# Pooled attention feeding a four-expert layer: two token blocks in one PSUM bank, double-buffered attention sums, an earlier q, plain products in the first chunk, merged last stores

## The chip, the cores and the metric

The kernel runs on one core of a Trainium2 chip. The metric is the device time of one execution in microseconds (us). Each experiment was timed beside runs of the kernel before on the same chip. Engines are named as the profile names them: PE is TensorE, PEld its weight loads, DVE is VectorE, ACT is ScalarE, POOL is GpSimd, SP is SyncE. A "q" behind an engine's name (SPq) is that engine issuing a DMA, and L452 is line 452 of that run's kernel. A DMA *lands* when the trace reports its completion. The *granted clock* is the share of its full speed at which TensorE was allowed to run, as the profile records it; 0.5 is called half clock here.

## The reference, cut to what matters

```python
# q, k, v: (8 batches, 8 heads, 576 tokens, 64)   x: (4608, 512)   w1: (4, 512, 1024)   w2: (4, 1024, 512)
k_p = k.reshape(B, H, 72, 8, D).mean(axis=3)          # keys and values pooled by 8: 72 of each
v_p = v.reshape(B, H, 72, 8, D).mean(axis=3)
attn = softmax(q @ k_p.T / sqrt(D))
x = (attn @ v_p).transpose(0, 2, 1, 3).reshape(4608, 512)
p = domain_probs / (domain_probs.sum(-1, keepdims=True) + 1e-09)
for e in range(4):
    out += p[:, e:e + 1] * (np.maximum(x @ w1[e], 0) @ w2[e])
```

The arithmetic of the four experts dwarfs the attention. The kernel walks through nine chunks of tokens: the first 512 tokens of each of the eight batches, then one chunk of all the remainders (8 times 64 tokens). Each chunk passes through four experts. One chunk and one expert make one *step*. While the experts work on chunk b, the attention of batch b+1 is mixed in as small *pieces*.

## The kernel before: the parts that matter here

The pools. PSUM has one attention buffer of two banks (`psum_a`), two banks for the up product, and four tags `o0` to `o3` of one bank each for the down product:

```python
hpool  = ctx.enter_context(tc.tile_pool(name="hpool", bufs=2))
psum_a = ctx.enter_context(tc.tile_pool(name="psum_a", bufs=1, space=bass.MemoryType.PSUM))
psum_h = ctx.enter_context(tc.tile_pool(name="psum_h", bufs=2, space=bass.MemoryType.PSUM))
psum_o = ctx.enter_context(tc.tile_pool(name="psum_o", bufs=1, space=bass.MemoryType.PSUM))
```

Per step the *up product* is 8 groups of four 512-column matmuls, each followed by a ReLU on ScalarE. The *down product* is a seven-product scheme (in the manner of Strassen): 56 matmuls of 256 columns in place of 32 of 512. It needs sums of the hidden values (`S1` to `S4`) and, once per expert, sums of the weights; VectorE makes both. VectorE also adds each product, weighted by the token's probability, into `acc`:

```python
def weight_sums(e):                       # four VectorE instructions, in the first chunk
    combine(t[:, 0], b12, ALU.subtract, b11)
    combine(b12, b22, ALU.subtract, b12)
    combine(t[:, 1], b22, ALU.subtract, t[:, 0])
    combine(t[:, 2], b21, ALU.subtract, t[:, 1])

def down(c, e, step):                     # step 0..6: one of the seven products, two token blocks each
    ...
    for j in range(BANKS):
        tag = f"o{int(chain[1]) + j}"     # each token block has its own bank
        if not grows:
            state[tag] = psum_o.tile([P, NT], F32, tag=tag, name="o_ps")
        o_ps = state[tag][:, 0:HD]
        for i in range(HF):
            nc.tensor.matmul(o_ps, lhsT=lhs[:, i, j * P:(j + 1) * P], rhs=rhs[:, i, :],
                             start=(not grows and i == 0), stop=(i == HF - 1), ...)
        ...
        nc.vector.scalar_tensor_tensor(out=dst, in0=o_ps, scalar=prob, in1=dst,
                                       op0=ALU.mult, op1=ALU.add)     # right after its block
        if e == E - 1 and step in (5, 6):
            store(c, r)

def store(c, r):
    if c < B:
        ...
    else:                                 # the last chunk: two batches of 64 tokens in each block
        for bb in range(2):
            at = (2 * r + bb) * S + NT
            nc.sync.dma_start(out=out[at:at + REM, :], in_=acc[bb * REM:(bb + 1) * REM, r, :])
```

The start. TensorE runs filler matmuls on zeros (`idle`) while it waits for k and q, both cast to bf16 on the way by software DMA from GpSimd:

```python
load_k(0); load_q(0); load_v(0); load_w1(0); load_probs(); load_w1(1); ...    # all on GpSimd

def attention_first():
    idle(14)
    sum_keys(lo)
    idle(2)
    keys(0, lo)
    idle(8)
    sum_keys(hi)
    idle(2)
    keys(0, hi)
    for pair in range(NPAIR):
        queries(0, pair)
        if pair:
            scores(0, pair - 1)
    ...
```

The attention pieces of later batches end with the turn of x into the layout that the up product reads, by DMA transpose; the loads of the next batch are issued by GpSimd once the keys of this one are there (`gate`):

```python
def turn(b, r):
    if b:
        nc.sync.dma_start_transpose(out=state[("xT", b)][:, :, r * P:(r + 1) * P], in_=x_tok)
        return
    ...                                   # batch 0: four transposes on TensorE, copied by ScalarE

def next_loads(b):
    nc.gpsimd.tensor_copy(out=gate[0:1, 0:1], in_=state[("kpT", b)][0:1, 0, 0:1])
    load_q(b + 1); load_k(b + 1); load_v(b + 1); load_q_rem(b + 1)
```

The main loop, one step after the other: the up product of step s beside the down product of step s−1.

```python
for s in range(len(steps) + 1):
    ...
    for i in range(FCH):
        if 0 < s < len(steps):
            up(c, e, (i,))
        if s > 0 and i < 7:
            down(*steps[s - 1], i)
        slot()                            # now and then: one attention piece
        if s < len(steps) and i == HF:
            early_sum(c, e)
        if (s, i) in ((0, 6), (1, 5), (3, 0), (3, 6)):
            weight_sums(...)
```

The softmax here doesn't subtract the row's maximum and nothing guards it: scores larger than these inputs give would overflow.

Of the kernel before, what the change touches and what calls it, by code (L numbers as in the profile page):

```python
# [9 lines left out]
ACT = mybir.ActivationFunctionType  # L10
ALU = mybir.AluOpType
# [6 lines left out]
def kernel(  # L18
# [36 lines left out]
    hpool = ctx.enter_context(tc.tile_pool(name="hpool", bufs=2))  # L55
    spool = ctx.enter_context(tc.tile_pool(name="spool", bufs=1))

    psum_a = ctx.enter_context(tc.tile_pool(name="psum_a", bufs=1, space=bass.MemoryType.PSUM))
# [35 lines left out]
    def load_q(b):  # L94
        q_sb = qpool.tile([P, H, NR, D], BF16, name="q_sb")
        for hs in groups(b):
            nc.gpsimd.dma_start(  # L97
                out=q_sb[:, hs].rearrange("p h r d -> p h (r d)"),
                in_=q[b, hs, 0:NT, :].rearrange("h (p r) d -> p h (r d)", r=NR),
            )  # L100
        raws[("q", b)] = q_sb
# [60 lines left out]
    def spare_bank():  # L162

        turns[0] += 1
        return psum_o.tile([P, NT], F32, tag=f"o{turns[0] % 4}", name="spare")
# [80 lines left out]
    def scores(b, pair):  # L246
        qT = state[("qT", b)]
        if pair == 0:
            state[("expT", b)] = apool.tile([SP, H, 2, 2, P], BF16, name="expT")
        expT = state[("expT", b)]  # L250
        banks = two_banks(b == 0 and pair % 2)
        for hh in range(2):
            h = 2 * pair + hh
            for r2 in range(2):
                lo = r2 * D
                nc.tensor.matmul(  # L256
                    banks[r2][:, hh * 2 * P:(hh + 1) * 2 * P],
                    lhsT=key_columns(b, h, lo), rhs=qT[lo:lo + D, h],
                )
        exp_out = expT[:, 2 * pair:2 * pair + 2].rearrange("j h a b t -> j b (h a) t")  # L260
        for sc, r2 in whole(banks):
            nc.scalar.activation(  # L262
                out=exp_out[:, r2], in_=sc[0:SP].rearrange("j b (g t) -> j b g t", t=P),
                func=ACT.Exp, scale=EXP_SCALE,
            )

    def one_bank(b):
        return spare_bank()[:] if b == 0 else two_banks(False)[0]

    def two_banks(spare):  # L270
        if spare:
            return [spare_bank()[:], spare_bank()[:]]
        t = psum_a.tile([P, 2, NT], F32, tag="a", name="a_ps")
        return [t[:, 0], t[:, 1], t]

    def whole(banks):

        if len(banks) == 3:
            return [(banks[2][:], slice(0, 2))]
        return [(banks[i].unsqueeze(1), slice(i, i + 1)) for i in range(2)]  # L280

    def divide(banks, x_tok):

        for ps, hs in whole(banks):
            n = hs.stop - hs.start
            c = ps[:, :, 0:NPAIR * (D + 1)].rearrange("p a (h d) -> p a h d", d=D + 1)
            inv = npool.tile([P, 2, NPAIR], F32, name="inv")
            nc.vector.reciprocal(out=inv[:, 0:n], in_=c[:, :, :, D])  # L288
            nc.vector.tensor_tensor(  # L289
                out=x_tok[:, hs], in0=c[:, :, :, 0:D],  # L290
                in1=inv[:, 0:n].unsqueeze(3).to_broadcast([P, n, NPAIR, D]), op=ALU.mult,
            )

    def context(b, r):
        expT, vp = state[("expT", b)], vps[b % 3]
        x_tok = npool.tile([P, 2, NPAIR, D], BF16, name="x_tok", bufs=4)
        banks = two_banks(b == 0 and r % 2)
        for h in range(H):
            at = h % NPAIR * (D + 1)
            nc.tensor.matmul(  # L300
                banks[h // NPAIR][:, at:at + D + 1],
                lhsT=expT[:, h, r // 2, r % 2, :], rhs=vp[:, h, :],
            )
        divide(banks, x_tok)
        state[("x", b, r)] = x_tok
# [40 lines left out]
    def rem_context(i):  # L346
        expTr = state.pop(("expTr", i))
        x_tok = npool.tile([P, 2, NPAIR, D], BF16, name="x_tok", bufs=4)
        banks = two_banks(False)
        for h in range(H):  # L350
            at = h % NPAIR * (D + 1)
            for bb in range(2):
                nc.tensor.matmul(  # L353
                    banks[h // NPAIR][bb * REM:(bb + 1) * REM, at:at + D + 1],
                    lhsT=expTr[:, h % 2, bb, h // 2, :], rhs=vps[(2 * i + bb) % 3][:, h, :],
                )
        divide(banks, x_tok)
        state[("xr", i)] = x_tok
# [7 lines left out]
    def attention_first():  # L366

        lo, hi = groups(0)
        idle(14)
        sum_keys(lo)  # L370
        idle(2)
        keys(0, lo)
        idle(8)
        sum_keys(hi)
        idle(2)
        keys(0, hi)
        for pair in range(NPAIR):
            queries(0, pair)
            if pair:
                scores(0, pair - 1)  # L380
        scores(0, NPAIR - 1)
        idle(1)
# [19 lines left out]
    def attention(b):  # L402
# [15 lines left out]
        for pair in range(NPAIR):  # L418
            pieces.append(lambda pair=pair: scores(b, pair))
# [48 lines left out]
    BANKS = 2  # L468
# [35 lines left out]
    def down(c, e, step):  # L504
# [3 lines left out]
        if step == 0:  # L508
            hidden_sums(c, e)
        chain, grows, lhs, rhs, row, col, first = [  # L510
            lambda: ("o0", 0, a11, w[:, LO, 0:HD], 0, 0, True),
            lambda: ("o2", 0, a12, w[:, HI, 0:HD], 0, 0, False),
            lambda: ("o0", 1, state["S2"], t[:, 1], 0, 1, True),
            lambda: ("o2", 0, state["S1"], t[:, 0], 1, 1, True),
            lambda: ("o0", 1, state[("S3", c, e)], w[:, LO, HD:DM], 1, 1, False),
            lambda: ("o2", 1, state["S4"], w[:, HI, HD:DM], 0, 1, False),
            lambda: ("o0", 1, a22, t[:, 2], 1, 0, True),
        ][step]()
        for j in range(BANKS):
            tag = f"o{int(chain[1]) + j}"  # L520
            if not grows:
                state[tag] = psum_o.tile([P, NT], F32, tag=tag, name="o_ps")
            o_ps = state[tag][:, 0:HD]
            for i in range(HF):
                nc.tensor.matmul(  # L525
                    o_ps, lhsT=lhs[:, i, j * P:(j + 1) * P], rhs=rhs[:, i, :],
                    start=(not grows and i == 0), stop=(i == HF - 1),
                    skip_group_check=True,
                )
            r = row * BANKS + j  # L530
            prob = p_all[:, c * NR + r, e:e + 1]
            dst = acc[:, r, col * HD:(col + 1) * HD]
            if e == 0 and first:
                nc.scalar.activation(out=dst, in_=o_ps, func=ACT.Copy, scale=prob)  # L534
            else:
                nc.vector.scalar_tensor_tensor(  # L536
                    out=dst, in0=o_ps, scalar=prob, in1=dst, op0=ALU.mult, op1=ALU.add,
                )
            if e == E - 1 and step in (5, 6):
                store(c, r)  # L540
        if step == 1:
            last_sum(c, e)

    def store(c, r):
# [3 lines left out]
        else:  # L548
            for bb in range(2):
                at = (2 * r + bb) * S + NT  # L550
                nc.sync.dma_start(out=out[at:at + REM, :],
                                  in_=acc[bb * REM:(bb + 1) * REM, r, :])
# [11 lines left out]
    steps = [(c, e) for c in range(NCH) for e in range(E)]  # L564
    SLOTS = E * FCH


    ENG = mybir.EngineType
    with tc.manual_schedule(engines={ENG.PE, ENG.DVE, ENG.Activation, ENG.Pool, ENG.SP}):
        load_k(0)  # L570
        load_q(0)
        load_v(0)
        load_w1(0)
        load_probs()
        load_w1(1)
        load_w2(0)
        load_w1(2)
        load_w2(1)
        attention_first()
# [3 lines left out]
        load_w1(3)  # L583
# [16 lines left out]
        for s in range(len(steps) + 1):  # L600
            if s < len(steps):
                c, e = steps[s]
                if e == 0:
                    while pieces:
                        pieces.popleft()()
                    pieces.extend(attention(c + 1) if c + 1 < B else
                                  rem_pieces(c // 2) if c < B else [])

                    late = SLOTS // 2 - 1 if c == 0 else 0
                    per_slot = len(pieces) / (SLOTS - 3 - late)  # L610
                    due = -late * per_slot
            for i in range(FCH):
                if 0 < s < len(steps):
                    up(c, e, (i,))
                if s > 0 and i < 7:
                    down(*steps[s - 1], i)
                slot()
                if s < len(steps) and i == HF:
                    early_sum(c, e)

                if (s, i) in ((0, 6), (1, 5), (3, 0), (3, 6)):
                    weight_sums({(0, 6): 0, (1, 5): 1, (3, 0): 2, (3, 6): 3}[(s, i)])
# [30 lines left out]
```

## Time and profile before

| quantity | value | read from |
|---|---|---|
| device time, median | 539.25 us (538.17 to 540.45, 4 runs) | times |
| span of the profiled run, mean granted clock | 537.5 us, 0.992 | list of cores |
| PE busy | 516.9 us, 96% | page, part 1 |
| start of the first up product | 22.17 us | timeline |
| second up product to second chunk | 30.58 to 84.16 us | trace, first weight load of each up product |
| last accumulate ends, span ends | 530.92, 537.5 us | timeline |

The profile page of the kernel before: busy time, the granted clock in 40 equal slices, and the chain of work that ended last.

```profile
span 537.5 us, 9393 instructions
...
PE 516.9 (96%) x3839; PEld 335.5 (62%) x3839; DVE 365.2 (68%) x745; ACT 238.3 (44%) x413; POOL 41.6 (8%) x59
...
PEclk9999989999999999999999999999999999999998
...
PE 85%; DMA 8%; DVE 4%; POOL 1%; ACT 1%; issue 0%; DVEq 0%; POOLq 0%
```

TensorE bounds the kernel. The windows view of the same kernel says where. Its columns are the stretch (start and end, length), busy us and instructions of PE, PEld, DVE, ACT and POOL, then the granted clock, the mean number of busy DMA packets divided by 16 engines (packets overlap, so it can pass 1), and GB/s.

```profile
8.00:16.00 8.00, 6.62 (x61) 3.75 (x59) 2.98 (x8) 2.44 (x5) 3.63 (x6) 1.00 1.28 188
16.00:24.00 8.00, 6.93 (x84) 5.56 (x81) 5.44 (x17) 4.46 (x10) 3.37 (x5) 1.00 1.18 213
71.77:75.19 3.42, 1.50 (x18) 0.92 (x16) 3.39 (x9) 0.00 (x0) 0.00 (x0) 1.00 1.70 101
75.19:78.61 3.42, 3.42 (x14) 1.82 (x12) 1.67 (x4) 0.60 (x1) 0.00 (x0) 0.50 1.40 105
84.50:140.40 55.90, 55.90 (x434) 35.98 (x432) 42.16 (x85) 26.64 (x45) 3.84 (x5) 1.00 0.51 85
140.40:195.30 54.90, 54.90 (x402) 35.60 (x400) 39.26 (x79) 25.88 (x45) 4.43 (x5) 1.00 0.41 69
195.30:251.10 55.80, 55.80 (x433) 35.99 (x432) 40.28 (x81) 26.92 (x45) 3.44 (x5) 1.00 0.50 83
531.00:537.50 6.50, 0.00 (x0) 0.00 (x0) 0.00 (x0) 0.00 (x0) 0.00 (x0) 0.62 0.69 160
```

Three chunks in the middle keep PE busy every microsecond at full clock. Only the ends have slack: the start, the first chunk (with one stretch at half clock, right after a stretch in which PE was busy 1.50 of 3.42 us), and the tail, in which only DMA works, at a busy share of 0.69.

What TensorE waits for in the whole run of the kernel before (waiting engine, tile and line, then what it waited for, us in total, times, longest):

```profile
PE a_ps L300 <- DVE x_tok L289: 1.9, 1, 1.9
PE a_ps L237 <- DMA q_sb<-in_q_dram: 1.8, 1, 1.8
PE a_ps L237 <- DVE qT L240: 1.8, 2, 1.3
```

The first three stand in the first chunk; two of them exist because the attention sums have one buffer. The timeline of the kernel before, four rows from start and end (start, us, engine and line, what; in brackets the idle time before it and what ended that):

```profile
1.20 6.00 PE L215 MATMUL w_ps<-zeros 128*128 128x512 bf16 x14 [1.20 <-DVE zeros L556]
7.04 1.04 PE L199 MATMUL s_ps<-kraw,ident 72*72 72x256 bf16 x8
...
22.17 1.03 PE L452 MATMUL h_ps<-xT,w_bf 128*128 128x256 bf16 x8 [0.41 <-ACT xT L318]
...
529.77 5.03 SPq L551 DMA_DIRECT2D out_dram<-acc  x8
```

At the end SyncE needs 5.03 us to issue eight stores.

### The profile page before, as it was taken

How to read it: one execution, taken by the hardware profiler on the slowest of the kernel's cores; microseconds unless marked ns; L12 is line 12 of the kernel's file. 1: busy time of each engine (PE TensorE's matmuls, PEld its weight loads, DVE VectorE, ACT ScalarE, POOL GpSimd, SP SyncE). 2: the span in 40 equal slices, each digit the busy share in tenths (PEclk: the TensorE clock that was granted, in tenths of full speed). 3: DMA queues.
4: the chain of work that ended last, by engine and by line, in shares of the span. 5: the costliest groups of instructions: out<-in, count | busy, mean ns of one | idle time of the engine just before them, and what ended most of it. 6: DMA issues, size and time to landing. Idle time of an engine off the chain costs nothing.

```text
span 537.5 us, 9393 instructions
## 1 busy us (share of the span) xinstructions
PE 516.9 (96%) x3839; PEld 335.5 (62%) x3839; DVE 365.2 (68%) x745; ACT 238.3 (44%) x413; POOL 41.6 (8%) x59
## 2 busy tenths in 40 slices
PE   8897989999999999999999999999999999999993
PEld 4664556666665666566656665666566666666663
DVE  2548678867775778477937785778477636763665
ACT  1662523563356335633473347333743364336330
POOL 7410200200030000200300002000000000000000
PEclk9999989999999999999999999999999999999998
DMA  8999993491265134913491329331001110011003
GB/s 124 209 208 206 201 113 60 111 123 31 50 142 82 29 61 91 136 28 59 102 124 21 68 78 129 49 60 59 32 15 27 45 44 2 11 39 40 2 1 78
DMA packets 73419, 41.52 MB, mean 77 GB/s; under 512 B 44688, under 2 KB 67216, under 8 KB 73376
## 3 DMA queue, kind: packets, MB, share of 16 engines
q0 software_dynamic: 32032, 22.63, 29.7%
q1 hardware_dynamic: 41344, 18.29, 15.3%
q8 instruction: 30, 0.49, 0.4%
q14 instruction: 13, 0.11, 0.1%
HBM read 45.16 MB, written 9.44 MB: 102 GB/s over the span
## 4 chain that ended last, share of the span: by engine, by line
PE 85%; DMA 8%; DVE 4%; POOL 1%; ACT 1%; issue 0%; DVEq 0%; POOLq 0%
PE h_ps L452 43%; PE o_ps L525 38%; DMA kraw<-in_k_dram 4%; DMA w_bf<-in_moe_w_dram 3%; PE a_ps L256 2%; PE a_ps L300 1%; DVE acc L536 1%; DMA x_rem<-x_tok 0%; ACT expT L262 0%; DVE wt_bf L471 0%; POOL q_sb L97 0%; PE a_ps L353 0%; POOL kraw L89 0%; POOL vraw L89 0%; DVE x_tok L289 0%
## 5 line engine op out<-in xcount | busy, mean ns | idle before, releaser
L456 ACT ACTIVATE H_sb<-h_ps 128x512 bf16<-128x512 f32 (+1 forms) x296 | 173.2, 585 | 253.1 <-PE h_ps L452 252.7
L452 PE MATMUL h_ps<-xT,w_bf 128*128 128x512 bf16 (+1 forms) x1056 | 260.4, 374 | 0.7 <-ACT xT L318 0.4
L536 DVE SCALAR_TENSOR_TENSOR acc<-o_ps,p_all,acc 128x256 f32<-128x256 f32 x432 | 194.1, 481 | 96.0 <-PE o_ps L525 78.6
L452 PEld LDWEIGHTS <-w_bf 128*128 128x128 bf16 x1184 | 110.9, 98 | 86.8 <-issue 8.0
L525 PEld LDWEIGHTS <-H_sb 128*128 128x128 bf16 x864 | 84.5, 98 | 32.5 <-DMA w_bf<-in_moe_w_dram 0.4
L525 PE MATMUL o_ps<-w_bf,H_sb 128*128 128x256 bf16 x576 | 74.5, 273 | 0.0
L525 PE MATMUL o_ps<-wt_bf,H_sb 128*128 128x256 bf16 x288 | 37.3, 273 | 0.0
L262 ACT ACTIVATE expT<-a_ps 72x1024 bf16<-72x1024 f32 x30 | 30.5, 1017 | 13.7 <-PE a_ps L256 13.7
L452 PE MATMUL h_ps<-x_rem,w_bf 128*128 128x512 bf16 x128 | 32.4, 379 | 0.8 <-DMA x_rem<-x_tok 0.8
L534 ACT ACTIVATE acc<-o_ps,p_all 128x256 f32<-128x256 f32 x72 | 31.3, 472 | 3.9 <-DMA out_dram<-acc 3.4
L289 DVE TENSOR_TENSOR x_tok<-a_ps,inv 128x512 bf16<-128x512 f32 x34 | 23.5, 691 | 1.2
L300 PEld LDWEIGHTS <-expT 72*128 72x128 bf16 x256 | 12.3, 98 | 4.4 <-DVE x_tok L289 2.2
L215 PE MATMUL w_ps<-zeros 128*128 128x512 bf16 x31 | 10.8, 489 | 1.2 <-DVE zeros L556 1.2
L429 POOL COPY gate<-kpT_101 1x1 bf16<-1x1 bf16 x2 | 1.4, 708 | 102.1 <-DMA kpT_101<-kp_99 55.5
L288 DVE RECIPROCAL inv<-a_ps 128x8 f32<-128x8 f32 x34 | 6.7, 198 | 3.5 <-PE a_ps L300 3.1
L168 DVE TENSOR_TENSOR kraw<-kraw 72x2048 bf16<-72x2048 bf16 x7 | 8.5, 1212 | 0.3 <-DMA kraw<-in_k_dram 0.3
L168 DVE TENSOR_TENSOR vraw<-vraw 72x2048 bf16<-72x2048 bf16 x7 | 8.5, 1211 | 0.0
L429 POOL COPY gate<-kpT_103 1x1 bf16<-1x1 bf16 x2 | 1.9, 934 | 84.8 <-DMA kpT_103<-kp_100 45.2
L300 PE MATMUL a_ps<-vp_105,expT 72*128 72x65 bf16 x96 | 5.1, 194 | 3.0 <-DVE x_tok L289 1.9
L97 POOL DMA_DIRECT2D q_sb<-in_q_dram x9 | 7.8, 868 | 1.4 <-issue 1.1
L89 POOL DMA_DIRECT2D kraw<-in_k_dram x9 | 7.6, 842 | 3.9 <-DMA p_all<-in_moe_domain_probs_dram 3.4
L89 POOL DMA_DIRECT2D vraw<-in_v_dram x9 | 7.3, 810 | 1.8 <-DVE vp_105 L220 1.8
(513 smaller groups left out, 484.8 us busy)
## 6 DMA issues: line engine op xcount, KB each, us to landing
out_dram<-acc SPq DMA_DIRECT2D x32, 256.0 KB, 2.6
w_bf<-in_moe_w_dram POOLq DMA_DIRECT2D x7, 1024.0 KB, 23.8
kraw<-in_k_dram POOLq DMA_DIRECT2D x7, 576.0 KB, 11.6
vraw<-in_v_dram POOLq DMA_DIRECT2D x7, 576.0 KB, 13.4
q_sb<-in_q_dram POOLq DMA_DIRECT2D x7, 512.0 KB, 8.3
w_bf<-in_moe_w_dram POOLq DMA_DIRECT2D x2, 512.0 KB, 13.0
out_dram<-acc SPq DMA_DIRECT2D x8, 128.0 KB, 2.3
kraw<-in_k_dram POOLq DMA_DIRECT2D x2, 288.0 KB, 5.8
```

The source lines that it names most:

```text
L89: nc.gpsimd.dma_start(out=raw[:, hs], in_=src[b, hs].rearrange("h (j r) d -> j h r d", r=POOL))
L168: nc.vector.tensor_add(out=raw[:, hs, 0:4, :], in0=raw[:, hs, 0:4, :], in1=raw[:, hs, 4:8, :])
L215: nc.tensor.matmul(w_ps[:], lhsT=zeros[:, 0:P], rhs=zeros[:])
L256: nc.tensor.matmul(banks[r2][:, hh * 2 * P:(hh + 1) * 2 * P], lhsT=key_columns(b, h, lo), rhs=qT[lo:lo + D, h],)
L262: nc.scalar.activation(out=exp_out[:, r2], in_=sc[0:SP].rearrange("j b (g t) -> j b g t", t=P), func=ACT.Exp, scale=EXP_SCALE,)
L289: nc.vector.tensor_tensor(out=x_tok[:, hs], in0=c[:, :, :, 0:D], in1=inv[:, 0:n].unsqueeze(3).to_broadcast([P, n, NPAIR, D]), op=ALU.mult,)
L300: nc.tensor.matmul(banks[h // NPAIR][:, at:at + D + 1], lhsT=expT[:, h, r // 2, r % 2, :], rhs=vp[:, h, :],)
L452: nc.tensor.matmul(out_ps, lhsT=w1_bf[:, e, kc, fc * P:(fc + 1) * P], rhs=xT[:, kc, at], start=(kc == 0), stop=(kc == KC - 1),)
L456: nc.scalar.activation(out=H_sb[:, fc, at], in_=out_ps, func=ACT.Relu)
L525: nc.tensor.matmul(o_ps, lhsT=lhs[:, i, j * P:(j + 1) * P], rhs=rhs[:, i, :], start=(not grows and i == 0), stop=(i == HF - 1), skip_group ...
L534: nc.scalar.activation(out=dst, in_=o_ps, func=ACT.Copy, scale=prob)
L536: nc.vector.scalar_tensor_tensor(out=dst, in0=o_ps, scalar=prob, in1=dst, op0=ALU.mult, op1=ALU.add,)
```

## The change

Its intent: free the two PSUM banks that the attention needs for a second buffer, by letting two token blocks of the down product share a bank; bring q in early by the hardware queue; take the seven-product scheme, with its sums, out of the crowded first chunk; and end with four stores on two queues instead of eight on one. The diff, cut to its core:

```diff
-    hpool = ctx.enter_context(tc.tile_pool(name="hpool", bufs=2))
+    hpool = ctx.enter_context(tc.tile_pool(name="hpool", bufs=3))
-    psum_a = ctx.enter_context(tc.tile_pool(name="psum_a", bufs=1, ...))
+    psum_a = ctx.enter_context(tc.tile_pool(name="psum_a", bufs=2, ...))
 ...                                          # q of batch 0: f32 into acc by SyncE, then cast
+        wide = acc[:].rearrange("p r (g t) -> p (r g) t", t=NR * D)
         for hs in groups(b):
-            nc.gpsimd.dma_start(out=q_sb[:, hs]..., in_=q[b, hs, 0:NT, :]...)
+            nc.sync.dma_start(out=wide[:, hs], in_=src[:, hs])
+        for pair in range(NPAIR):
+            copy = nc.scalar.copy if pair % 2 else nc.vector.tensor_copy
+            copy(out=q_sb[:, hs]..., in_=wide[:, hs])
 ...                                          # two_banks()/spare banks go; every sum is one psum_a tile
     def attention_first():
-        idle(14)
+        idle(10)
         sum_keys(lo)
+        queries(0, 0)
+        keys(0, lo)
+        queries(0, 1)
         idle(2)
-        keys(0, lo)
-        idle(8)
         sum_keys(hi)
 ...
-        for pair in range(NPAIR):
-            pieces.append(lambda pair=pair: scores(b, pair))
+        for pair in range(0, NPAIR, 2):
+            pieces.append(lambda pair=pair: (scores(b, pair), scores(b, pair + 1)))
+            pieces.append(lambda: None)
 ...                                          # down(): both blocks of a product in one bank
-        for j in range(BANKS):
-            tag = f"o{int(chain[1]) + j}"
+        for j in range(BLOCKS):
+            o_ps = state[chain][:, j]
             for i in range(HF):
-                    start=(not grows and i == 0), ...
+                    start=(not grows and i == 0 and j == 0), ...
+        for j in range(BLOCKS):              # accumulates only after both blocks
+            add(state[chain][:, j], c, e, r, ...)
 ...
+    def down_plain(c, e, r):                 # first chunk: 8 matmuls of 512 columns, one accumulate
 ...                                          # store() of the last chunk
-            for bb in range(2):
-                at = (2 * r + bb) * S + NT
-                nc.sync.dma_start(out=out[at:at + REM, :],
-                                  in_=acc[bb * REM:(bb + 1) * REM, r, :])
+            queue = nc.sync if r % 2 else nc.scalar
+            queue.dma_start(
+                out=out.rearrange("(b s) d -> b s d", s=S)[2 * r:2 * r + 2, NT:S, :],
+                in_=acc[:, r, :],
+            )
 ...
+        load_q(0)
         load_k(0)
-        load_q(0)
 ...                                          # first chunk: down products one step later
+    steps = [((0, 0), None), ((0, 1), None), ((0, 2), (0, 0)), ((0, 3), (0, 1)), (None, (0, 2))]
 ...
-                if (s, i) in ((0, 6), (1, 5), (3, 0), (3, 6)):
-                    weight_sums(...)
+                if s in (5, 6) and i in (3, 6):      # the first two steps of the second chunk
+                    weight_sums(2 * (s - 5) + i // 6)
```

## The prediction

> **What bounds it now.** TensorE. The page gives PE busy 516.9 of 537.5 us (96%); the chain of waits is 85% PE. In the windows view the three chunks from 84.5 to 251.1 us have PE busy 166.6 of 166.6 us at granted clock 1.00, and the chain spaces four 512-column matmuls 0.865 us apart: 216 ns each[...]. So nothing can be won in the middle; only start, first chunk and end have slack.
>
> - First real matmul at 22.17 us (timeline).
> - First chunk: from the second expert (31.8) to the second chunk (84.5) 52.7 us pass, for about 26+13 us of expert work and 5 us of attention. The waits view shows why: q of batch 1 lands late (1.8 us), single-buffered attention sums (1.8+1.9+1.1 us on qT, x_tok, expT), weight sums (0.5+0.5), and a half-clock stretch around 75 to 79 us (eight 256-column matmuls take 1.7 us, not 0.87).
> - End: last accumulate ends at 530.9, but SyncE issues eight stores one after another, about 0.63 us each, so the last is issued at 534.2 and lands at 536.6.
>
> **What the change does.**
> - Start: q leaves the GpSimd queue, so v and w1 are issued 1.5 us earlier; sums double buffered; fewer idle matmuls. First real matmul near 21.0: gain 1.2 us (estimate).
> - First chunk: down products move one step later and are plain: 32 512-column matmuls (6.9 us) instead of 56 256-column ones (6.05 us), +0.85 us for each of 4 experts. PE work from the second up product to the second chunk becomes 6.9+13.8+13.8+6.9 plus 4 us attention = 45.4. I add 4 us of new waits: contexts follow the last scores at once with no matmul between (two 1.02 us exps), queries on qT copies, and x transposes at the chunk boundary. Gain about 3 us; then the fourth plain product runs beside the second chunk: −0.9.
> - Weight sums (16 adds of 0.69 us) move into the second chunk, on top of folds: DVE is oversubscribed for two steps. −1 us.
> - Middle: accumulates now start after both blocks, and the next matmuls on that bank wait for both. I measured the margin between the second accumulate and the matmuls that reuse its chain: usually over 1 us, but −0.3 us at three chunk borders and 0.2 at three more. About 0.3 us lost at each: −1. [...]
> - End: accumulates 0.7 us later by the same wait, but four stores on two queues instead of eight on one: +2.2 net.
>
> **Prediction.** Sum about 4 us: 535.7 us, range 532.3 to 538.6. Faster by over 2%: 0.03; within 2%: 0.95; slower: 0.02.
>
> **What would show it.** First real matmul near 21; second chunk starting near 79 to 82 rather than 84.5; small waits of o_ps on DVE at chunk borders; later chunk periods unchanged near 55 us; span minus last accumulate falling from 6.6 to about 4 us.
>
> **What would make it wrong.** Faster: my waits in the first chunk do not occur, nor the half-clock stretch (up to 4 us more). Slower: q as f32 delays k and v on the shared DMA engines; DVE backlog in the second chunk stalls PE for several us; bank sharing costs a wait in every step rather than at borders.

The terms are +1.2 (start), +3 and −0.9 (first chunk, fourth plain product), −1 (weight sums), −1 (middle) and +2.2 (end): 3.5 us, the "about 4" of the prediction, and 539.25 less that is its 535.7. That nothing can be won in the middle rests on the 166.6 of 166.6 us busy at a granted clock of 1.00; that 216 ns a matmul is the least possible is not shown.

## The result, and the profile after

| kernel | median | range, runs | ratio to before (95%) |
|---|---|---|---|
| before | 539.25 us | 538.17 to 540.45, 4 | |
| after | 569.57 us | 568.69 to 570.19, 4 | 1.0561 (1.0533 to 1.0588) |

All runs were correct, also with one start flag for the two blocks that share a bank (the diff sets it for the first block only). Executions over 1.5% slower than the fastest of the same kernel are left out of the means. A ratio here is the mean time of one kernel's fast runs over that of the other's in the same rounds, so it is not quite the ratio of the medians. The kernel became 5.6% slower; the prediction was a gain of 0.7%.

First, where the 30.7 us of the two spans came from. Each boundary is the first weight load of an up product, read from the two traces; the last column is what the prediction's terms imply.

| stretch | before, us | after, us | difference | predicted |
|---|---|---|---|---|
| span start to first up product | 21.57 | 27.99 | +6.42 | −1.2 |
| first up product | 9.01 | 10.68 | +1.67 | 0 |
| second up product to second chunk | 53.58 | 52.86 | −0.72 | −3 |
| first two steps of the second chunk | 28.55 | 34.61 | +6.06 | +1.9 |
| from there to the last up product | 396.64 | 396.49 | −0.15 | +1 |
| last up product to the end | 28.15 | 45.54 | +17.39 | −2.2 |

The middle, which holds nearly all the work and nearly all the bank sharing, did not change. The loss sits in the places where the prediction saw slack to be won.

The same parts of the page, for the changed kernel:

```profile
span 568.2 us, 9047 instructions
...
PE 524.3 (92%) x3730; PEld 332.7 (59%) x3730; DVE 339.3 (60%) x691; ACT 240.5 (42%) x409; POOL 41.7 (7%) x57
...
PEclk7589997999999999999999999999999999999975
...
PE 82%; DVE 9%; DMA 3%; ACT 1%; issue 1%; DVEq 0%; POOL 0%; POOLq 0%
```

PE has fewer instructions than before (3730 against 3839) but is busy longer, 524.3 us: some ran at half clock. The slices show three dips: the start, the boundary of the first two chunks, and the end. The chain's shares add up to 96%, where they added up to 99% before: the missing piece is the tail, which the chain does not follow back.

The windows view of the changed kernel, columns as before:

```profile
4.89:8.30 3.41, 0.44 (x2) 0.11 (x1) 0.59 (x2) 0.98 (x2) 2.94 (x4) 1.00 1.10 168
8.30:32.19 23.89, 22.00 (x140) 15.21 (x140) 8.82 (x22) 7.50 (x12) 8.90 (x11) 0.50 1.21 207
32.19:35.60 3.41, 3.24 (x30) 2.56 (x29) 0.00 (x0) 2.51 (x7) 0.69 (x1) 1.00 1.22 206
86.80:90.22 3.42, 0.00 (x0) 0.00 (x0) 0.16 (x1) 0.00 (x0) 0.00 (x0) 1.00 1.41 121
90.22:97.05 6.83, 5.49 (x13) 1.96 (x14) 0.00 (x0) 1.19 (x2) 0.00 (x0) 0.50 0.11 19
139.30:193.50 54.20, 54.14 (x400) 35.70 (x399) 38.47 (x79) 26.00 (x44) 4.47 (x5) 1.00 0.45 75
193.50:248.30 54.80, 54.22 (x425) 35.40 (x423) 38.55 (x79) 26.16 (x44) 3.65 (x5) 1.00 0.46 80
545.10:555.00 9.90, 0.00 (x0) 0.00 (x0) 0.00 (x0) 0.00 (x0) 0.00 (x0) 0.63 0.13 44
555.00:568.00 13.00, 0.00 (x0) 0.00 (x0) 0.00 (x0) 0.00 (x0) 0.00 (x0) 0.50 0.12 46
```

Line one: a 3.41 us stretch in which PE was busy 0.44 us. Line two: half clock for the 23.89 us that follow, with PE busy 22.00 of them. Line three: full clock again. Lines four and five: the wait for x, in which PE did nothing, and the 6.83 us of half clock after it. The last two: nothing but DMA for 23 us, at a share of 0.12 to 0.13 (2 of 16 engines would be 0.125), and 44 to 46 GB/s, against 0.69 and 160 GB/s in the tail of before.

What TensorE waits for in the changed kernel:

```profile
PE h_ps L443 <- DMA xT<-x_tok: 5.4, 1, 5.4
PE o_ps L514 <- DVE acc L546: 3.6, 5, 1.2
PE s_ps L205 <- DMA kraw<-in_k_dram: 3.0, 1, 3.0
...
PE o_ps L514 <- DVE S_989 L462: 1.3, 1, 1.3
```

The waits on attention sums of the kernel before are gone from the top. In their place stand k at the start, x of batch 1 at the chunk boundary, and VectorE in the second chunk. The timeline of the changed kernel, the rows that belong to these:

```profile
1.20 4.13 PE L221 MATMUL w_ps<-zeros 128*128 128x512 bf16 x10 [1.20 <-DVE zeros L564]
8.32 1.87 PE L205 MATMUL s_ps<-kraw,ident 72*72 72x256 bf16 x8 [2.98 <-DMA kraw<-in_k_dram]
...
28.46 1.87 PE L443 MATMUL h_ps<-xT,w_bf 128*128 128x256 bf16 x8 [0.23 <-ACT xT L308]
...
73.64 0.88 POOL L98 DMA_DIRECT2D q_sb<-in_q_dram  x1
...
79.48 6.93 SPq L303 DMA_TRANSPOSE xT<-x_tok  x4
...
91.56 3.57 PE L443 MATMUL h_ps<-xT,w_bf 128*128 128x512 bf16 x8 [5.39 <-DMA xT<-x_tok]
...
543.59 1.75 ACTq L557 DMA_DIRECT2D out_dram<-acc  x2
```

The fillers end at 5.33 and the first k lands at 8.28; in the kernel before it landed at 6.12, ahead of the fillers' end. The same eight 256-column matmuls take 1.87 us where they took 1.03. The last stores are issued by 545.6, yet the span ends at 568.2.

From this, four suspects: the store (about +17), the start with its half clock (about +8), the late x of batch 1, and the weight sums in the second chunk. For each, the theory and its rival:

- **Store.** Theory: the shape of the merged store, whose destination has an outermost dimension of 2, puts it on two DMA engines: the share of 0.13 in the tail, times the 16 engines of the page, is 2.1. That the outermost dimension does it is a supposition at this point. Rival: the second queue, on ScalarE, holds things up.
- **Start.** Theory: too few fillers let TensorE idle, and the clock falls. Rivals: q's early megabyte holds back k, so that fillers alone cannot help; or the new order of the start is slower in itself.
- **x of batch 1.** Theory: its transposes land late because the software loads of batch 2 are in flight. Rival: the attention of batch 1 simply ends too late.
- **Second chunk.** Theory: the weight sums of two steps on VectorE. Rivals: the half clock of the boundary, or the shared banks.

### The profile page after: what moved, and what is told of

The parts are those of the page before. It is cut to its first block, busy times and chain, and to the rows that moved or that the text cites. A ratio compares the mean times of both kernels' runs of the same rounds, so it can differ in the third digit from the quotient of the medians.

```text
span 568.2 us, 9047 instructions
## 1 busy us (share of the span) xinstructions
PE 524.3 (92%) x3730; PEld 332.7 (59%) x3730; DVE 339.3 (60%) x691; ACT 240.5 (42%) x409; POOL 41.7 (7%) x57
## 4 chain that ended last, share of the span: by engine, by line
PE 82%; DVE 9%; DMA 3%; ACT 1%; issue 1%; DVEq 0%; POOL 0%; POOLq 0%
PE h_ps L443 41%; PE o_ps L514 32%; PE o_ps L531 4%; DVE acc L546 3%; PE sc_ps L262 2%; PE c_ps L290 1%; PE s_ps L205 1%; DMA kraw<-in_k_dram 1%; DVE kraw L174 1%; DMA xT<-x_tok 1%; DVE kraw L176 1%; DVE wt_bf L462 1%; PE w_ps L221 1%; ACT expT L265 1%; DVE x_tok L279 0%
## 5 line engine op out<-in xcount | busy, mean ns | idle before, releaser
L546 DVE SCALAR_TENSOR_TENSOR acc<-o_ps,p_all,acc 128x256 f32<-128x256 f32 (+1 forms) x396 | 176.2, 487 | 153.4 <-PE o_ps L514 82.8
L514 PEld LDWEIGHTS <-H_sb 128*128 128x128 bf16 x768 | 75.1, 98 | 32.9 <-issue 4.9
L514 PE MATMUL o_ps<-w_bf,H_sb 128*128 128x256 bf16 x512 | 66.2, 273 | 2.5 <-DVE acc L546 2.4
L544 ACT ACTIVATE acc<-o_ps,p_all 128x256 f32<-128x256 f32 (+1 forms) x68 | 30.0, 483 | 16.8 <-PE o_ps L514 8.1
L514 PE MATMUL o_ps<-wt_bf,H_sb 128*128 128x256 bf16 x256 | 33.2, 272 | 0.3
L265 ACT ACTIVATE expT<-sc_ps 72x1024 bf16<-72x1024 f32 x32 | 30.8, 1014 | 5.7 <-PE sc_ps L262 5.6
L531 PE MATMUL o_ps<-w_bf,H_sb 128*128 128x512 bf16 x128 | 31.1, 389 | 0.0
L279 DVE TENSOR_TENSOR x_tok<-c_ps,inv 128x512 bf16<-128x512 f32 x36 | 24.9, 691 | 1.2
L531 PEld LDWEIGHTS <-H_sb 128*128 128x128 bf16 x128 | 12.6, 100 | 15.5 <-issue 1.9
L278 DVE RECIPROCAL inv<-c_ps 128x8 f32<-128x8 f32 x36 | 7.2, 199 | 4.2 <-PE c_ps L290 3.3
L205 PEld LDWEIGHTS <-ident 72*72 72x72 bf16 x32 | 5.8, 180 | 5.3 <-issue 4.5
```

Source lines behind the costliest of these rows:

```text
L205: nc.tensor.matmul(s_ps[0:SP, 0:n], lhsT=ident[:SP, :SP], rhs=raw[:, hs, r, :], start=(r == 0), stop=(r == POOL - 1))
L265: nc.scalar.activation(out=expT[:, 2 * pair:2 * pair + 2].rearrange("j h a b t -> j b (h a) t"), in_=sc_ps[0:SP].rearrange("j b h (a t) -> ...
L279: nc.vector.tensor_tensor(out=x_tok[:], in0=c[:, :, :, 0:D], in1=inv[:].unsqueeze(3).to_broadcast([P, 2, NPAIR, D]), op=ALU.mult,)
L531: nc.tensor.matmul(o_ps[:], lhsT=H_sb[:, fc, r * P:(r + 1) * P], rhs=w2_bf[:, e, fc, :], start=(fc == 0), stop=(fc == FCH - 1),)
L544: nc.scalar.activation(out=dst, in_=o_ps, func=ACT.Copy, scale=prob)
```

## The experiments

All twelve experiments gave correct results. Unless said otherwise an edit is made on the changed kernel. In the phases quoted, "first chunk" is the stretch from the second up product to the second chunk.

| run | what | median, us | ratio to before (95%) |
|---|---|---|---|
| after | the change | 569.57 | 1.0561 (1.0533–1.0588) |
| e1_store_rows | 64-row stores, two queues | 552.17 | 1.0250 (1.0229–1.0271) |
| e2_store_one_queue | merged stores, one queue | 569.24 | 1.0567 (1.0523–1.0610) |
| e3_idle22 | more fillers | 564.96, two groups | 1.0515 (1.0446–1.0584) |
| e5_q_gpsimd | q by GpSimd, new order | 569.05 | 1.0565 (1.0543–1.0587) |
| e7_start_old | start of before, weight loads left | 560.51 | 1.0420 (1.0386–1.0453) |
| e4_late_loads | loads of batch 2 later in the program | 569.26 | 1.0582 (1.0544–1.0621) |
| e4b_gate_on_x | loads of batch 2 held until x is there | 564.07 | 1.0473 (1.0443–1.0504) |
| e6_sums_early | weight sums spread | 566.30 | 1.0527 (1.0482–1.0572) |
| b1_store_merged | before, with the merged store | 556.17 | 1.0334 (1.0303–1.0365) |
| f3_four_mends | e1, e7, e4b and e6 together | 537.71 | 0.9978 (0.9954–1.0001) |
| f4_pe_turn | e1, e7, e6; x of batch 1 on TensorE | 536.68 | 0.9957 (0.9939–0.9976) |
| f5_staggered | f4 with contexts and turns staggered | 534.06 | 0.9913 (0.9892–0.9934) |

### The store: e1_store_rows, e2_store_one_queue, b1_store_merged

e1 takes back the shape and keeps the two queues:

```diff
-            queue.dma_start(out=out.rearrange("(b s) d -> b s d", s=S)[2 * r:2 * r + 2, NT:S, :],
-                            in_=acc[:, r, :])
+            for bb in range(2):
+                at = (2 * r + bb) * S + NT
+                queue.dma_start(out=out[at:at + REM, :], in_=acc[bb * REM:(bb + 1) * REM, r, :])
```

> The changed kernel with one part undone: the last four 256 KB stores are each written as two of 64 rows again, still on two queues. After the last accumulate (545.1 us) the changed kernel needed 23 us more, with a DMA share of 0.13, which is 2 of 16 engines. Theory A (the merged store's outer dimension is 2, so only 2 of the 16 DMA engines carry it): the stores land within 4 us of the last accumulate, the DMA share there is well above 0.13, time about 550 us (569.5 less 19 to 20). Rival B (the ScalarE queue, or two queues writing at once, is slow for stores): the tail stays near 23 us and the time near 569 us.

Measured: 552.17 us, all four runs within 0.6 us, 17.4 us less than the changed kernel by the medians. Its last accumulate ends at 545.09, as in the changed kernel (545.07), and its tail is 5.6 us. The windows view of e1, its tail:

```profile
545.10:550.70 5.60, 0.00 (x0) 0.00 (x0) 0.00 (x0) 0.00 (x0) 0.00 (x0) 0.70 0.62 176
```

A DMA share of 0.62 in place of 0.12, with the same bytes and the same two queues. The packets tell more than the share. The DMA view, first of the changed kernel from 545 to 568 us, then of e1 from 543.6 to 550.7:

```profile
DMA packets 518, 1.04 MB, mean 45 GB/s; under 512 B 8, under 2 KB 8, under 8 KB 518
DMA packets 640, 1.05 MB, mean 148 GB/s; under 512 B 128, under 2 KB 128, under 8 KB 640
```

The data packets have 2 KB in both. The small ones (4 bytes each in the trace) are two for each of the four merged stores and sixteen for each of the eight 64-row stores. Counted from the packets of the trace, two were in flight for 90% of the merged tail after 545.6 us; in e1 it was 13 to 17 for most of the time, and in the tail of the kernel before (eight stores of 64 rows) for 77% of it. An estimate from these counts is two engines for the merged stores and about sixteen for the others. The 256 KB stores of the earlier chunks, of 128 rows with no outermost 2, have sixteen small packets each as well and land 2.6 us after their issue (median, kernel before). e2 keeps the shape and takes back the queue:

```diff
-            queue = nc.sync if r % 2 else nc.scalar
+            queue = nc.sync
```

> The changed kernel with the merged stores kept, but all four on the SyncE queue. Theory A (2 of 16 engines by the shape of the store): nothing changes, DMA share 0.13 in the tail, landing 22 to 23 us after the last accumulate, time 569 us. Rival B (the second queue is the trouble): the tail shrinks to 4 to 6 us and the time to about 551 us.

Measured: 569.24 us (two runs), unchanged, with a DMA share of 0.12 to 0.13 in its tail:

```profile
543.20:553.00 9.80, 0.00 (x0) 0.00 (x0) 0.00 (x0) 0.00 (x0) 0.00 (x0) 0.62 0.13 45
```

So the queue does not matter and the shape does. b1 is the test from the other side: the kernel *before* with nothing but the merged store, on SyncE:

```diff
-            for bb in range(2):
-                at = (2 * r + bb) * S + NT
-                nc.sync.dma_start(out=out[at:at + REM, :], in_=acc[bb * REM:(bb + 1) * REM, r, :])
+            nc.sync.dma_start(out=out.rearrange("(b s) d -> b s d", s=S)[2 * r:2 * r + 2, NT:S, :],
+                              in_=acc[:, r, :])
```

> The kernel before with one part of the change alone: each of the last eight 64-row stores merged with its partner into one 128-partition store whose destination has outer dimension 2, all on the SyncE queue. Theory A (2 of 16 DMA engines): DMA share 0.13 in the tail, last landing about 22 us after the last accumulate instead of 5.7, time about 539 + 16 = 555 us. Rival (the merge alone saves issue time, as predicted): about 537 us.

Measured: 556.17 us, ratio 1.0334. The windows view of b1, its tail:

```profile
530.60:542.00 11.40, 0.00 (x0) 0.00 (x0) 0.00 (x0) 0.00 (x0) 0.00 (x0) 0.69 0.13 45
542.00:554.00 12.00, 0.00 (x0) 0.00 (x0) 0.00 (x0) 0.00 (x0) 0.00 (x0) 0.50 0.11 44
```

The merged store alone makes the kernel before 3.3% slower, and taking it back makes the changed kernel 3.1 points faster (1.0561 to 1.0250). The store is settled from both sides: the merged ones run at a share of 0.11 to 0.13, and 2 of 16 is 0.125. The runs compare an outermost dimension of 2 with 64 and 128 only; what other values would do is not shown.

### The start: e3_idle22, e5_q_gpsimd, e7_start_old

e3 only adds fillers, so that TensorE has work until k is there:

```diff
-        idle(10)
+        idle(22)
```

> The changed kernel with 22 filler matmuls at the start instead of 10 (before had 14). Theory A (TensorE stood 2.98 us for the late keys, the granted clock fell to 0.5 at 8.3 us and stayed there until 32.2, and that halves the attention and the first up products): no half clock before 32 us, first up product near 22 us instead of 28.5, that product 9 us instead of 10.7, time 8 us less, about 561.5. Rival B (the first up product is late because q's transfer delays k and v by 2 us and the attention chain waits on VectorE and ScalarE): first up product later than 26 us, time within 2 us of 569.5.

Measured: four runs in two groups, 560.83 and 562.09, and 567.83 and 569.45 (the last counted as slow and not used for the ratio). The profiled run, of 560.83, kept full clock through the start: its first up product begins at 22.24 us instead of 28.46. By the three fast runs full clock at the start is worth some 6 us (561.5 on average, against 567.83), and the fillers bring it in some executions and not in others. The slower group was not traced; that it lost the clock is read from the mean granted clock of its runs (0.964 and 0.958, against 0.977 and 0.975). But 22.24 is no better than the 22.17 of the kernel before: even where the clock holds, the new start gains nothing.

e5 takes q off the SyncE queue and keeps the new order and the ten fillers:

```diff
         if b: ...
+        for hs in groups(b):
+            nc.gpsimd.dma_start(out=q_sb[:, hs]..., in_=src[:, hs])
+        return
 ...
-        load_q(0)
         load_k(0)
+        load_q(0)
```

> The changed kernel with q of batch 0 loaded as before (GpSimd queue, cast in the DMA, after k), still with 10 filler matmuls. If q's move is what makes the keys late, k lands at 6.1 us again instead of 8.3, TensorE's wait at 5.3 us is under 1 us, the clock stays full, and the first up product comes near 21 to 22 us, time about 561 us. If the fewer filler matmuls alone cause it, the half clock stays (k still lands after 5.3) and the time stays within 2 us of 569.5.

Measured: 569.05 us, unchanged. The time is what the theory of the fillers expected, but the trace shows a route that I had not written down. k now lands early (its sums start at 6.13), but the new order wants q before the keys, and q comes late. The timeline of e5, and one stretch of its windows view:

```profile
6.13 1.03 PE L208 MATMUL s_ps<-kraw,ident 72*72 72x256 bf16 x8 [1.21 <-DMA kraw<-in_k_dram]
11.40 0.61 PE L246 MATMUL spare<-ident,q_sb 128*128 128x128 bf16 x4 [4.24 <-DMA q_sb<-in_q_dram]
...
4.05:7.46 3.41, 1.91 (x12) 1.07 (x10) 0.26 (x1) 0.00 (x0) 3.41 (x5) 1.00 0.93 135
```

TensorE waits 1.21 us for k and then 4.24 us for q instead of 2.98 us for k, and the clock is halved from 7.46, again for 23.89 us. It falls only 0.30 us into the wait for q, so the other 3.94 us of that wait are not what cost it. What went before it is a stretch of 3.41 us in which the ten fillers ran out and PE was busy 1.91 us. A late k is thus not needed to lose the clock. e7 puts back the start of the kernel before (the order of k and q, q by GpSimd, 14+2+8+2 fillers, keys before queries), and leaves the rest of the change, the new order of the weight loads included:

```diff
-        load_q(0)
         load_k(0)
+        load_q(0)
 ...                     # q by GpSimd as in e5, and
-        idle(10)
+        idle(14)
         sum_keys(lo)
-        queries(0, 0)
-        keys(0, lo)
-        queries(0, 1)
         idle(2)
+        keys(0, lo)
+        idle(8)
         sum_keys(hi)
 ...
```

> The changed kernel with the start as before: q of batch 0 by the GpSimd queue after k, 14 filler matmuls and the old order of queries, keys and scores; double-buffered attention sums stay. Theory A (the half clock from 8.3 to 32.2 us comes of the new start's idle TensorE, and costs about 8 us): clock full to the first chunk's end in every run, first up product at 22 us, time about 561.5 and steady from run to run (unlike the 22-filler kernel, whose runs fell in two groups, 561 and 569). If the double-buffered sums were at fault instead, the time stays near 569.

Measured: 560.51 us, four runs from 560.23 to 562.13, so steady. The first up product starts at 21.64, the first two stretches of the table are 21.04 and 9.01 us. So the start is undone as a whole; which part of it does it (fillers, order or q's queue) no run separates. The windows view of e7:

```profile
8.00:16.00 8.00, 6.39 (x59) 3.78 (x61) 2.65 (x7) 3.01 (x5) 3.75 (x6) 1.00 1.29 186
16.00:24.00 8.00, 7.04 (x85) 5.84 (x85) 4.17 (x10) 4.04 (x9) 2.25 (x3) 1.00 1.18 212
```

Here PE is busy 6.39 and 7.04 of 8 us at full clock, *less* than the 22.00 of 23.89 us that the changed kernel was busy at half clock (eight matmuls of 256 columns take 1.87 us there and 1.03 at full clock, so they fill more of the time). What share of busy time keeps the clock and what restores it are thus two different things in these runs.

The traces show a little more. The half-clock stretches in which TensorE had work lasted 3.41 us (the kernel before, from 75.19), 6.83 and 23.89 us (the changed kernel), 23.89 us (e5) and 20.48 us (e6): 1, 2, 7, 7 and 6 times 3.41 us. In the 3.41 us before the clock fell PE was busy 1.50 us (before), 0.44 us and 0 (the changed kernel, start and boundary), and 1.91 us (e5), so it need not have been idle. And a stretch of full work did not bring the clock back: in the changed kernel PE was busy 3.42 of 3.42 us between 21.95 and 25.37, and the clock stayed at half until 32.19 (in that stretch ran value sums, fillers and contexts, no transposes). Full clock came 3.73 us after the first up product began in the changed kernel (28.46), and 1.72 us after it in e5 (29.63). By what rule it falls and returns is not shown.

A caution on the mean granted clock that each run lists: one of the changed kernel's four runs has 0.975 with 568.69 us, the others 0.954 to 0.957. That does not show a full-clock start. In e4b's profiled run the mean is as high as 0.982, but its clock records begin only some 30 us into the span, and its matmuls before that run at half speed (the first eight of 256 columns take 1.86 us). The mean there counts the 30 us without a record as full clock. I did not trace the 568.69 run.

### x of batch 1: e4_late_loads, e4b_gate_on_x

In the changed kernel the four transposes of batch 1 are issued from 79.48 to 86.41 us; the trace gives no landing for them, but TensorE's wait for them ends at 91.56. The software loads of batch 2, issued from 73.64 on, land at 80.19, 85.07, 89.24 and 90.57. In the kernel before the first such transpose, issued at 67.34, also landed only at 78.54, when the loads beside it had landed (78.31 to 78.60), but there was slack to hide it. e4 moves the loads of batch 2 behind the last turn in the program:

```diff
-        pieces += [..., lambda: (fold_values(b, every), next_loads(b))]
+        pieces += [..., lambda: (fold_values(b, every), next_loads(b) if b > 1 else None)]
 ...
+        if b == 1:
+            pieces.append(lambda: next_loads(b))
```

> The changed kernel, with the loads of q, k, v of batch 2 issued after the last x transpose of batch 1 instead of before its contexts. In the changed kernel the four DMA transposes of x, issued at 79.5 to 86.4 us, land only when those loads have drained (91 us), and TensorE waits 5.4 us and then runs 6.8 us at half clock. Theory A (the transposes are held up behind the software loads on the shared DMA engines): each transpose lands about 1.2 us after its issue ends, the 5.4 us wait is under 1 us, no half clock near 90 us, time 7 to 8 us less: about 562. Rival B (four transposes close together are slow in themselves): the wait stays above 3 us and the time within 2 us of 569.5.

Measured: 569.26 us, and a miss of my own making. GpSimd ran through its own instructions as soon as its gate let it (gate at 72.51, first load at 73.56); the later place in the program did not hold it back. The loads were issued at 73.56 instead of 73.64: nothing was tested. e4b keeps that edit and also ties the gate to the data:

```diff
-        nc.gpsimd.tensor_copy(out=gate[0:1, 0:1], in_=state[("kpT", b)][0:1, 0, 0:1])
+        nc.gpsimd.tensor_copy(out=gate[0:1, 0:1], in_=state[("kpT", b)][0:1, 0, 0:1] if b > 1
+                              else state[("xT", b)][0:1, 0, NT - 1:NT])
```

> The changed kernel, with the loads for batch 2 made to wait for the last x transpose of batch 1. (The run e4_late_loads only moved their place in the program: the GpSimd queue ran ahead and still issued them at 73.6 us, so it tested nothing.) Theory A (the transposes are held up behind the software loads on the shared DMA engines): each transpose lands about 1.2 us after its issue ends, the 5.4 us wait of TensorE falls under 1.5 us, no half clock near 90 us, time 6 to 8 us less than 569.5: about 562.5. Rival B (four transposes close together are slow in themselves): the wait stays above 3 us, the time within 2 us of 569.5.

Measured: 564.07 us, 5.5 us less by the medians and 4.7 by the ratios, where 6 to 8 were expected. The timeline of e4b:

```profile
86.02 0.18 POOL L422 COPY gate<-xT 1x1 bf16<-1x1 bf16 x1 [45.57 <-DMA xT<-x_tok]
...
102.86 1.03 PE L517 MATMUL o_ps<-w_bf,H_sb 128*128 128x256 bf16 x8 [1.93 <-DVE acc L549]
```

The last transpose now has landed by 86.02. The wait for x falls from 5.4 to 0.8 us and the half clock after it is gone; the first chunk takes 48.31 us instead of 52.86, the next step 13.63 instead of 16.32. The step after that takes 20.59 instead of 18.29: k of batch 2 now comes late, VectorE waits for it, and TensorE for VectorE (1.93 us and two shorter waits). So the theory holds, the rival (attention simply too late) is left with 0.8 of the 5.4 us, and part of the gain is given back one step later.

### The second chunk: e6_sums_early

```diff
-                if s in (5, 6) and i in (3, 6):
-                    weight_sums(2 * (s - 5) + i // 6)
+                if (s, i) in ((3, 0), (4, 7), (5, 3), (6, 6)):
+                    weight_sums({(3, 0): 0, (4, 7): 1, (5, 3): 2, (6, 6): 3}[(s, i)])
```

> The changed kernel, with the weight sums spread out: one while the plain products of the third expert start, one at the end of the plain-only step, one in each of the two steps that had two. Theory A (VectorE is oversubscribed where the second chunk starts, TensorE's waits of 1.2 and 1.3 us there and the 19.2 us of the second step against 14.9 before come from the sums): the second step falls to about 16 us, the waits go, time 2.5 to 4 us less, about 566.5. Rival B (that step is long for the arrangement of two blocks in a bank, which makes accumulates start later): the step stays above 18 us.

Measured: 566.30 us; the intervals of its ratio and that of the changed kernel overlap, so the total alone does not settle it. The trace does for the step in question: the second step of the second chunk takes 15.63 us instead of 18.29, and the waits of TensorE on VectorE there (1.2 and 1.3 us) are gone. In this profiled run the half clock of the start also lasted 20.48 us instead of 23.89, and the two stretches of the start were 1.8 us shorter; that part of its gain is not the edit's.

### All together, and a better version: f3_four_mends, f4_pe_turn, f5_staggered

f3 is e1, e7, e4b and e6 in one kernel; it keeps the bank sharing, the double-buffered sums and the plain first chunk.

> The changed kernel with the four mends together: old start, stores of 64 rows on two queues, loads for batch 2 after the x transposes of batch 1, weight sums spread. If the costs add as measured one by one (-17.3 store, -9 start, -6 to -7 loads, -3 sums from 569.3) the time is 533 to 534.5 us, about 1% under before. If they overlap or the late loads stall VectorE in the second chunk, 536 to 541.

Measured: 537.71 us, ratio 0.9978 (0.9954 to 1.0001). The single undos took 3.11, 1.41, 0.88 and 0.34 points off 1.0561; added, that leaves 0.9987. Within the noise the four undos take the whole loss away, and by the ratios they add. In us I had written 533 to 534.5 for costs that add, and 536 to 541 for overlap or for a stall by the late loads; 537.71 lies in the second range, and the trace shows the stall: the second step of the second chunk takes 19.36 us, against 15.63 in e6. The ratios add all the same because e4b's own already holds this stall (20.59 us). In f3 the transposes of batch 1, with no software load in flight, landed 1.2 us after their issue ended (72.57 to 73.78, and so on); of the 28 in the kernel before the median is 1.19 us of issue and 2.4 us from issue to landing.

f4 replaces the gate by another way out: x of batch 1 is turned on TensorE, as that of batch 0, so nothing waits for a DMA at the boundary and the loads of batch 2 keep their early place.

```diff
-        if b:
+        if b > 1:
             nc.sync.dma_start_transpose(out=dst, in_=x_tok)
             return
-        xt_ps = spare_bank()[:]...
+        xt_ps = one_bank(b)...
```

> As the kernel with four mends, but the loads for batch 2 are issued where the changed kernel has them, and the x transposes of batch 1 are made on TensorE and copied by ScalarE, so that they need no DMA. TensorE does 16 more 128-column transposes (about 1 us) and never waits for these transposes. Theory A (the loads are all that held up the second chunk): second chunk starts within 1.5 us of where it starts with four mends, time within 1.5 us of that kernel, 532.5 to 535.5. If the loads hold up the second chunk by another way too (queries or keys of batch 2), this kernel is the slower by more than 2 us.

Measured: 536.68 us, ratio 0.9957. The second chunk starts at 81.84, 3.0 us later than in f3 (78.81), where I had expected at most 1.5; its first two steps take 29.45 us instead of 32.99. Between 50 and 90 us TensorE still waits 2.6 us for x_tok before the turns and 1.5 us for exponentials before the contexts. f5 puts each turn one place later, behind the next context, spreads the pieces of batch 1 over more slots, and moves the first weight sum by four slots:

```diff
-                begin(1, 2 * FCH - 3, 2)
+                begin(1, 2 * FCH - 2)
 ...
+        if b == 1:
+            for r in range(NR):
+                pieces.append(lambda r=r: context(b, r))
+                if r:
+                    pieces.append(lambda r=r: turn(b, r - 1))
+            pieces += [lambda: None, lambda: turn(b, NR - 1)]
+            return pieces
 ...
-                if (s, i) in ((3, 0), (4, 7), (5, 3), (6, 6)):
+                if (s, i) in ((3, 4), (4, 7), (5, 3), (6, 6)):
```

> As the kernel with four mends and TensorE transposes, but the attention of batch 1 in the first chunk starts two slots earlier, an up product and a plain down product stand between its last scores and its first context, and each x transpose is issued one context later. That kernel (536.7 us) still had TensorE waits of 1.5 us (contexts on exps) and 2.6 us (transposes on x_tok) there. If those waits are what is left of the first chunk's loss, they fall under 1 us together and the time is about 533 us, 1% under before. If VectorE, which has the folds, the weight sums and the divides in the same stretch, just moves the waits elsewhere, the time stays within 1 us of 536.7.

Measured: 534.06 us (533.52 to 534.57, 6 runs) against 538.95, ratio 0.9913 (0.9892 to 0.9934), clear of 1. The waits of TensorE in f5 between 48 and 90 us, three of them in all:

```profile
PE c_ps L293 <- ACT xT L311: 0.7, 1, 0.7
PE sc_ps L265 <- ACT expT L268: 0.5, 1, 0.5
PE a_ps L310 <- ACT xT L311: 0.4, 1, 0.4
```

By the table of stretches, f5 against the kernel before: start 20.99 (−0.6), first up product 9.01 (0), first chunk 48.11 (−5.5), two steps of the second chunk 29.45 (+0.9), middle 396.49 (−0.15), end 27.69 (−0.5). The whole gain sits in the first chunk. It is not the gain of the change alone: f5 also turns x of batch 1 on TensorE and staggers it, and the change with its four losses mended (f3) is level with before.

## Why the prediction was wrong, point by point

The prediction was 535.7 us (532.3 to 538.6); the kernel took 569.57. What bounds the kernel it had right (TensorE, nothing to win in the middle). Four terms of its sum were too good, and a fifth, the middle, was too bad.

- **"End: accumulates 0.7 us later by the same wait, but four stores on two queues instead of eight on one: +2.2 net."** This step failed most: the stretch lost 17.4 us. I costed the issue (eight times about 0.63 us, right) and took the transfer for granted, as if 1 MB would move at the same rate in any shape. The runs show that the shape decides: 5.6 us of tail with 64-row stores and 23 us with the merged ones, on the same queues (e1, e2), and the same loss on the kernel before (b1). This alone would have moved the prediction above its range.
- **"First real matmul near 21.0: gain 1.2 us."** It came at 28.46. The prediction counted "fewer idle matmuls" as a gain. They were not all slack: with 22 of them the profiled run of e3 kept full clock through the start. Ten end at 5.33 us, k lands at 8.3 because q's megabyte goes first, and the 2.98 us wait is followed by 23.89 us of half clock. "q as f32 delays k and v on the shared DMA engines" was named among what would make it wrong, but as a delay; k did land 2.2 us later (8.28 instead of 6.12), but in e5, with k back at 6.09, the clock was lost with ten fillers too (23.89 us at half). e7 undid the loss; e3 showed that without it the new start is at 22.24, level with before.
- **"Gain about 3 us"** in the first chunk. The term was 0.7 as run, 5.3 with x held up no longer (e4b), 5.5 in f5. With the plain products and the double buffer the waits on q, qT and x_tok of before are gone, which is worth more than I gave them; how much each of the two gave no run separates. What ate the gain was a wait that the prediction named only in passing, "x transposes at the chunk boundary", inside a lump of 4 us: it was 5.4 us, plus 6.83 us of half clock behind it. Its cause was not in the prediction: the transposes were held up while the loads of batch 2 were in flight (e4b).
- **"DVE is oversubscribed for two steps. −1 us."** The mechanism was right, its size was off: the second of the two steps lost 2.8 us (15.53 to 18.29), and spreading the sums took 2.7 us of that back (e6). The first of them lost 3.3 us (13.02 to 16.32), mostly to the half clock of the boundary, as e4b's 13.63 shows; the 0.9 us I put there for the fourth plain product is what f5 still pays.
- **Middle, "About 0.3 us lost at each: −1."** It was nothing: −0.15 us over 396 us. TensorE does wait for `acc` at some borders (3.6 us in five waits over the whole run), but the chunks of the middle are as short as before: 54.14 of 54.20 and 54.22 of 54.80 us busy.

And the chances: 0.95 on "within 2%" was too sure. It rested on small terms, each with a small error. The three largest misses came from a *state* that switches (a DMA share of 0.13 or 0.62, a granted clock of 0.50 or 1.00, loads in flight or not), and such errors are not small; only the weight sums were a matter of size.

## What to carry to other kernels

When DMAs are merged to save issues, look at the outermost dimension of the destination before counting: stores of 2 times 64 rows had two packets in flight and a DMA share of 0.13, and four of them cost 23 us; eight stores of 64 rows had a share of 0.62 and cost 5.6 (e1). Filler matmuls ahead of the first data are not just slack: with ten of them the start ran 23.89 us at half clock (the changed kernel, e5), with 22 the profiled run of e3 not at all. So cut them only if the data comes earlier, and give a change of load order a look at what lands *later* for it (k at 8.28 us instead of 6.12). And when a wait is measured at a boundary, ask what else is in the DMA engines at that moment: hold loads back by a data dependence (e4b, issued from 86.53 us), as the place in the program did not do it (e4, 73.56 instead of 73.64).
